# One dummy product per step on TensorE, from step 9 to step 54 of the attention of group 0

## The chip, the cores and the metric

The kernel runs on one NeuronCore of a Trainium2 chip. The metric is the device time of one execution in microseconds (us); lower is better. The kernel before takes 572.56 us, the median of three runs (572.24 to 572.80).

## The reference

Three blocks follow one another.

1. Causal attention over 2 batches, 12 heads, 448 positions and 64 values per head: `scores = q kT / 8`, the upper triangle masked, `exp(scores - max)` divided by its row sum, times `v`. The result becomes `x`, 896 tokens by 768.
2. `h = x @ w_in` (768 to 2048), `g = h * clip(h + 3, 0, 6) / 6`, `x = g @ w_out` (2048 to 768).
3. RMS norm of `x` with a gain vector, then `silu(xn @ w_gate) * (xn @ w_val)` (768 to 1536 twice) and `@ w_out` (1536 to 768).

The weights come as 64-bit floats; the products have to be as good as 32-bit ones.

## The kernel before, in words

The sequence is cut in two halves of 224 positions. Group 0 is the first half of all sequences, group 1 the second. Attention works in units of two heads of one batch: units 0 to 11 are group 0 (112 x 224 scores at most), units 12 to 23 are group 1 (112 x 448 at most). After attention a product is written as three: high half times high half, high times low, low times high (`mm3`, lines 209, 211 and 213), each 128 x 128 weights by 448 columns.

The order of all instructions is written out by hand in *steps*. In each step the loop at the end of the kernel first issues what has come due (`due`: masks, exponentials, evictions, each so many steps after what it needs), then the entries of `plan` for this step in order of their priority number, then some products of the dense layers. The products start at step 67 (`products_from`) and only then; so TensorE, which works in program order, comes to the first of them when everything of steps 0 to 66 is done. Engines do not stop between steps: a step is only a place in the order.

Unit `u` starts at step `5 u`. The stages of a unit of group 0, by line:

- **s** (line 319, TensorE): four score products, each in two passes, so eight matmul rows. Two heads use the upper and the lower 64 rows of the array. Entry `a_scores` at step 5u.
- mask and row minimum (329, VectorE), two steps later; **exp** and row sums (336, ScalarE), two steps after that; reciprocal of the sums (343, 344, VectorE); scaling (354, GpSimd).
- **t** (370, TensorE): three transposes of 112 x 112 for each of two heads, entry `a_transpose` at steps 5u + 15 and 5u + 16.
- **pt** (380, ScalarE): the copy of a transposed tile out of PSUM.
- **o** (396, TensorE): four products with `v` in eight passes, entry `a_values` at step 5u + 22; then the split of the result (406 ScalarE, 412 VectorE).

Units 8 to 11 have shorter distances (tables `SUMS`, `TRANSPOSES`, `VALUES`, `LAG`), so that the last value products of group 0 are at step 64. From step 23 on, five steps of group 0 hold on TensorE: t and s, then t, then o, then two steps with nothing. ScalarE also prepares the first weights in this time: `narrowed` (line 160) and `w_halves` (185) from steps 26, 38 and 50.

All results of TensorE go through one pool of eight PSUM banks (`psum`). One of its tiles is `warm`: `warm_up(n)` (line 933) issues n products of a 128 x 128 tile of ones by itself into it, and nothing reads it. Before, it is called six times over at the very start and once at each of steps 1, 3, 6 and 8. A bank goes back to the pool when the last instruction that uses its tile is issued in the written order.

Of the kernel before, what the change touches and what calls it, by code (L numbers as in the profile page):

```python
# [51 lines left out]
def fused_kernel(ctx: ExitStack, tc, qa, qb, ka, kb, v, w_in, w_out, w_gate, w_val, w_out2, rms_g, out):  # L52
# [13 lines left out]
    def psum(name):  # L66
        return pspool.tile([128, 512], F32, tag="ps", name=name)
# [27 lines left out]
    def begin_step():  # L95
        now = clock["now"]
        while due[now]:
            fn, args = due[now].pop(0)
            fn(*args)
        del due[now]  # L100

    def end_step():
        clock["now"] += 1
# [167 lines left out]
    NA = NU // 2  # L271
    ld, lv, sm, st, pt, xs = {}, {}, {}, {}, {}, {}

    def phase(u):
        return {NA - 1: 2, NU - 1: 2, NA - 2: 3, NA - 3: 4, NA - 4: 5}.get(u, units[u][0])
# [637 lines left out]
    def products():  # L913
        yield from ff1_in(0, 0)
        plan_preps(0, *PREPS[0])
        yield from ff1_in(1, NP1)
        yield from ff1_out(0, 2 * NP1)
        at(1, w_split)
        plan_preps(PREPS[0][2], *PREPS[1])
        pair_early(PLAIN)  # L920
        yield from ff1_out(1, 3 * NP1)
        yield from ff2_plain(IN2)
        yield from ff2_strassen()
        yield from strassen(OUT2)

    with tc.manual_schedule():
        nc.vector.memset(ones, 1.0)

        warm = psum("warm")

        def warm_up(n):
            for _ in range(n):
                nc.tensor.matmul(warm[:, :128], ones, ones, start=True, stop=True)

        warm_up(6)
        make_identity(nc, ident)
        nc.gpsimd.memset(mask, 0.0)
        nc.gpsimd.affine_select(
            out=mask[:, S - C:], in_=mask[:, S - C:], compare_op=ALU.is_ge, fill=MASK,
            base=0, pattern=[[-1, C]], channel_multiplier=1)  # L940
        nc.gpsimd.memset(half, 0.5)
        nc.gpsimd.memset(eps, 1e-6)


        plan = defaultdict(list)

        def start(u):
            return 5 * u

        for n in (1, 3, 6, 8):  # L950
            plan[n].append((4, warm_up, 1))
        for u in range(NU):
            s0 = start(u)
            ahead = max(0, NA + 4 - u) if u >= NA else 0
            plan[max(0, s0 - (24 if u < NA else 6 + 4 * ahead))].append((0, a_load, u))
            t0, o0 = s0 + TRANSPOSES[phase(u)], s0 + VALUES[phase(u)]
            plan[o0 - 12].append((0, a_load_v, u))
            plan[s0].append((3, a_scores, u))
            for j in range(2):
                plan[t0 + j].append((3, a_transpose, u, j))  # L960
            plan[o0].append((3, a_values, u))
        products_from = max(start(u) + VALUES[phase(u)] for u in range(NA)) + 3
        plan[0].append((1, lambda: nc.sync.dma_start(gvec, rms_g.rearrange("(k p) -> p k", p=128))))
        for n in range(3):
            plan[12 + 12 * n].append((1, w_load))
            plan[52 + 6 * n].append((1, w_load))
        for n in range(3):
            plan[26 + 12 * n].append((0, w_split))

        work = products()  # L970
        live = True
        attention_until = max(start(u) + VALUES[phase(u)] for u in range(NU)) + 3
        quota = 0.0
        while live or any(plan.values()) or any(due.values()):
            begin_step()
            now = clock["now"]
            for _, fn, *args in sorted(plan.pop(now, []), key=lambda e: e[0]):
                fn(*args)
            if now >= products_from and live:
                quota += BESIDE if now < attention_until else AFTER  # L980
                while quota >= 1 and live:
                    quota -= 1
                    if next(work, 0) == 0:
                        live = False
            end_step()
# [56 lines left out]
```

## Time and profile before

| | |
|---|---|
| median of three runs | 572.56 us |
| the profiled execution | 572.75 us |
| its span, first to last instruction | 571.0 us |
| mean granted TensorE clock | 0.996 of full |
| TensorE busy (matmul rows) | 562.2 us, 98% of the span |
| VectorE busy | 410.4 us, 72% |
| ScalarE busy | 390.6 us, 68% |
| GpSimd busy | 85.5 us, 15% |

All views come from one profiled execution. A timeline row gives the start and the length of a merged run of like instructions. Matmul rows overlap: the end of one is modelled and reaches past the start of the next, so what a group costs TensorE is best read from start to next start. PE is TensorE's matmul, PEld its weight load, DVE VectorE, ACT ScalarE, POOL GpSimd, SPq the DMA queue of SyncE. A clock of 1.00 is 2.4 GHz and 0.50 is 1.2 GHz. The share of busy time hides that the kernel has stages: up to about 47 us there is attention of group 0 alone, and afterwards dense products, with attention of group 1 in between.

### The profile page before, as it was taken

Reading aid. Unit: us, or ns where it says so; the run is one execution under the profiler, and the core shown is the slowest. Engines: PE = TensorE matmul, PEld = TensorE weight load, DVE = VectorE, ACT = ScalarE, POOL = GpSimd, SP = SyncE. Lnnn points to the kernel's source line nnn. Section 1 sums busy time; section 2 is a strip of 40 time slices with the busy share of each in tenths; the row PEclk is TensorE's granted clock in tenths of the full one; section 3 lists DMA queues with packets and bytes.
Section 4 is the critical chain, followed back from the end, with each engine's and each line's share of the span. In section 5 each row is a group of like instructions: output and inputs, shape, how many; then the busy total and the mean of one; then the engine's idle time right before and its main releaser. Section 6 shows DMA issues by size and latency. Waiting matters only on the chain.

```text
span 571.0 us, 9072 instructions
## 1 busy us (share of the span) xinstructions
PE 562.2 (98%) x3048; PEld 491.8 (86%) x3048; DVE 410.4 (72%) x796; ACT 390.6 (68%) x766; POOL 85.5 (15%) x130
## 2 busy tenths in 40 slices
PE   8899999999999999999999999999999999999997
PEld 6556777777899999999999999999999999999996
DVE  4676686867558857555589869969886876966861
ACT  6997878787667766877487767486667664754430
POOL 4665636362200000001001100000000000000000
PEclk9999999999999999999999999999999999999999
DMA  8958767664266997997789923037744607585841
GB/s 226 275 155 280 232 224 228 212 215 142 64 238 211 318 357 259 322 344 257 265 292 383 398 106 143 10 118 264 260 157 179 223 33 260 184 280 198 274 145 64
DMA packets 51231, 125.59 MB, mean 220 GB/s; under 512 B 6768, under 2 KB 30256, under 8 KB 51184
## 3 DMA queue, kind: packets, MB, share of 16 engines
q1 hardware_dynamic: 50752, 124.66, 63.6%
q8 instruction: 24, 0.39, 0.3%
q10 hardware_dynamic: 432, 0.34, 0.2%
q14 instruction: 23, 0.19, 0.1%
HBM read 93.36 MB, written 31.62 MB: 219 GB/s over the span
## 4 chain that ended last, share of the span: by engine, by line
PE 95%; ACT 3%; DMA 1%; SPq 0%; issue 0%; DVE 0%
PE y L209 8%; PE y L213 8%; PE y L211 8%; PE h L213 7%; PE h L209 7%; PE h L211 7%; PE f L209 5%; PE f L213 5%; PE f L211 5%; PE s L319 4%; PE o L396 4%; PE t L370 4%; PE fx L209 2%; PE fr L213 2%; PE fx L213 2%; PE fr L211 2%
## 5 line engine op out<-in xcount | busy, mean ns | idle before, releaser
L191 DVE TENSOR_TENSOR wlo<-c,whi 128x768 fp32r<-128x768 f32 x89 | 88.9, 1003 | 19.7 <-ACT whi L185 18.0
L185 ACT CAST whi<-c 128x768 fp32r<-128x768 f32 x89 | 74.0, 834 | 37.9 <-DVE c L169 18.0
L213 PE MATMUL h<-xh,wlo 128*128 128x448 f32 x192 | 72.0, 375 | 0.0
L211 PE MATMUL h<-xl,whi 128*128 128x448 f32 x192 | 70.9, 369 | 0.0
L209 PE MATMUL y<-ghi,whi 128*128 128x448 f32 x192 | 70.6, 367 | 0.0
L209 PE MATMUL h<-xh,whi 128*128 128x448 f32 x192 | 70.4, 367 | 0.0
L213 PE MATMUL y<-ghi,wlo 128*128 128x448 f32 x192 | 70.0, 365 | 0.0
L211 PE MATMUL y<-glo,whi 128*128 128x448 f32 x192 | 69.3, 361 | 0.0
L354 POOL TENSOR_SCALAR sm<-sm,st 112x112 f32<-112x112 f32 (+1 forms) x96 | 55.6, 598 | 69.3 <-ACT pt L380 28.3
L336 ACT ACTIVATE sm<-sm,st 112x112 f32<-112x112 f32 (+3 forms) x96 | 49.8, 530 | 4.3 <-DVE st L329 4.3
L169 DVE SCALAR_TENSOR_TENSOR c<-c,raw 128x768 uint32<-128x768 uint32 x36 | 36.5, 1015 | 17.4 <-ACT raw L164 10.7
L213 PEld LDWEIGHTS h<-xh,wlo 128*128 128x128 f32 x192 | 36.0, 188 | 9.3 <-issue 6.7
L329 DVE CUSTOM_DVE_ANT_0 sm<-s,mask 112x112 f32<-112x112 f32 (+3 forms) x96 | 37.3, 442 | 7.9 <-PE s L319 7.6
L433 DVE SCALAR_TENSOR_TENSOR t<-t,h 128x448 f32<-128x448 f32 x32 | 19.7, 616 | 27.1 <-ACT t L429 27.0
L213 PEld LDWEIGHTS y<-ghi,wlo 128*128 128x128 f32 x192 | 35.9, 187 | 3.6 <-issue 0.2
L211 PEld LDWEIGHTS h<-xl,whi 128*128 128x128 f32 x192 | 36.0, 188 | 2.8
L211 PEld LDWEIGHTS y<-glo,whi 128*128 128x128 f32 x192 | 36.0, 188 | 2.7
L209 PEld LDWEIGHTS h<-xh,whi 128*128 128x128 f32 x192 | 36.2, 188 | 2.5
L209 PEld LDWEIGHTS y<-ghi,whi 128*128 128x128 f32 x192 | 36.0, 188 | 2.5 <-issue 0.2
L429 ACT ACTIVATE t<-h,half 128x448 f32<-128x448 f32 x32 | 20.4, 636 | 25.3 <-PE h L213 25.3
L370 PE MATMUL t<-ident,sm 112*112 112x112 f32 x240 | 32.9, 268 | 2.7 <-POOL sm L354 2.3
L600 POOL TENSOR_TENSOR sq<-sq,sq 128x448 f32<-128x448 f32 x8 | 10.1, 1258 | 170.1 <-ACT sq L589 164.5
(174 smaller groups left out, 1351.9 us busy)
## 6 DMA issues: line engine op xcount, KB each, us to landing
raw<-in_w_in SPq DMA_DIRECT2D x16, 768.0 KB, 5.4
raw<-in_w_out SPq DMA_DIRECT2D x16, 768.0 KB, 6.3
braw<-in_w_out SPq DMA_DIRECT2D x12, 768.0 KB, 6.1
c<-kept SPq DMA_DIRECT2D x21, 384.0 KB, 3.1
a<-left SPq DMA_DIRECT2D x35, 224.0 KB, 3.9
praw<-in_w_gate SPq DMA_DIRECT2D x10, 768.0 KB, 4.5
praw<-in_w_val SPq DMA_DIRECT2D x10, 768.0 KB, 5.9
keptin<-c SPq DMA_DIRECT2D x16, 384.0 KB, 2.7
```

The source lines that it names most:

```text
L169: nc.vector.scalar_tensor_tensor(bits, bits, 3, z, ALU.logical_shift_left, ALU.bitwise_or)
L185: nc.scalar.copy(hi, c)
L191: nc.vector.tensor_sub(lo, c, f32(hi))
L209: nc.tensor.matmul(ps, whi, xhi, start=first, stop=False, skip_group_check=again)
L211: nc.tensor.matmul(ps, whi, xlo, start=False, stop=False, skip_group_check=again)
L213: nc.tensor.matmul(ps, wlo, xhi, start=False, stop=last, skip_group_check=again)
L319: nc.tensor.matmul(ps[:C, o:o + n], tq[64 * j:64 * j + 64, i * C:(i + 1) * C], tk[64 * j:64 * j + 64, 0:n], start=True, stop=True)
L329: nc.vector.tensor_tensor_reduce(dst, src, mask[:, S - n:], scale=-0.125, scalar=3e38, op0=ALU.add, op1=ALU.min, accum_out=st[u][:, 0, c:c ...
L336: nc.scalar.activation(dst, dst, AF.Exp, scale=-1.0, bias=st[u][:, 0, c:c + 1], accum_out=st[u][:, 1, c:c + 1])
L354: nc.gpsimd.tensor_scalar(t[:, o:o + n], t[:, o:o + n], c, 1.0, op0=ALU.mult, op1=ALU.mult)
L370: nc.tensor.transpose(banks[-1][:C, o:o + C], t[:, o0 + kc * C:o0 + (kc + 1) * C], ident[:C, :C])
L396: nc.tensor.matmul(ps[64 * j:64 * j + 64, HS - n:HS], tv[:, kc, 64 * j:64 * j + 64], t[:, o:o + n], start=kc == 0, stop=kc == nk - 1)
```

## The change

`warm_up(1)` is planned once more at each of steps 9 to 54 (`start(NA - 1)` is 55), 46 times in all, with priority 2: after the loads of its step and before its score, transpose and value products (priority 3).

```diff
         for n in (1, 3, 6, 8):
             plan[n].append((4, warm_up, 1))
+        for n in range(9, start(NA - 1)):
+            plan[n].append((2, warm_up, 1))
         for u in range(NU):
```

Nothing else is edited. The tile `warm` is now used until step 54 rather than step 8, and so is its PSUM bank.

## Rows read from the trace of the kernel before

**Rows 1.** Page: busy time by engine, and the chain of waits by engine.
```profile
PE 562.2 (98%) x3048; PEld 491.8 (86%) x3048; DVE 410.4 (72%) x796; ACT 390.6 (68%) x766; POOL 85.5 (15%) x130
PE 95%; ACT 3%; DMA 1%; SPq 0%; issue 0%; DVE 0%
```

**Rows 2.** Busy time by stage: engines (x instructions), clock, DMA share, GB/s.
```profile
8.18:34.14 25.96, 22.66 (x184) 14.14 (x183) 18.64 (x106) 25.92 (x101) 18.41 (x41) 0.93 0.81 241
34.14:47.05 12.91, 11.93 (x90) 7.22 (x90) 8.71 (x34) 11.27 (x41) 8.38 (x16) 1.00 0.79 238
47.05:571.00 523.95, 520.49 (x2744) 464.77 (x2742) 381.28 (x644) 350.10 (x617) 57.20 (x65) 1.00 0.63 219
27.66:31.07 3.41, 3.41 (x20) 2.00 (x19) 2.45 (x16) 3.41 (x15) 1.97 (x6) 0.50 0.76 220
```

**Rows 3.** Waits of TensorE, whole run: us in total, times, longest.
```profile
PE t L370 <- POOL sm L354: 2.3, 3, 1.4
PE o L396 <- DMA v<-in_v: 0.4, 1, 0.4
PE s L319 <- ACT pt L380: 0.2, 1, 0.2
```

**Rows 4.** Timeline of TensorE, group 0 at full clock: start, length, what.
```profile
11.93 0.83 PE L319 MATMUL s<-k,q 64*112 64x112 f32 x8
12.69 0.50 PE L370 MATMUL t<-ident,sm 112*112 112x112 f32 x3
13.12 0.79 PE L396 MATMUL o<-pt,v 112*64 112x224 f32 x8
13.85 0.50 PE L370 MATMUL t<-ident,sm 112*112 112x112 f32 x3
14.28 0.83 PE L319 MATMUL s<-k,q 64*112 64x112 f32 x8
```

**Rows 5.** The tile of the dummy products, whole run: ns min/median/max.
```profile
L933 PEld LDWEIGHTS warm<-ones x20: 186/333/334, 1.0 to 7.9; 128*128 128x128 f32 x20
L933 PE MATMUL warm<-ones x20: 275/421/582, 1.0 to 8.0; 128*128 128x128 f32 x20
```

**Rows 6.** Timeline of weight loads: two dummy products, then scores, full clock.
```profile
7.54 0.52 PEld L933 LDWEIGHTS warm<-ones 128*128 128x128 f32 x4 [0.29 <-issue]
...
8.18 0.37 PEld L319 LDWEIGHTS s<-k,q 64*112 64x112 f32 x6
```

**Rows 7.** Timeline of weight loads: last transpose of seven, then dense products.
```profile
48.45 0.14 PEld L370 LDWEIGHTS t<-ident,sm 112*112 112x112 f32 x1
48.55 0.19 PEld L211 LDWEIGHTS h<-xl,whi 128*128 128x128 f32 x1
48.66 0.19 PEld L213 LDWEIGHTS h<-xh,wlo 128*128 128x128 f32 x1
```

**Rows 8.** Timeline of TensorE around the dense products' start.
```profile
47.76 0.37 PE L209 MATMUL h<-xh,whi 128*128 128x448 f32 x1
47.97 0.84 PE L370 MATMUL t<-ident,sm 112*112 112x112 f32 x7
```

**Rows 9.** Timeline of TensorE, units 10 to 13: scores, the first dense product.
```profile
31.50 0.83 PE L319 MATMUL s<-k,q 64*112 64x112 f32 x8
...
34.14 0.83 PE L319 MATMUL s<-k,q 64*112 64x112 f32 x8
...
44.92 1.57 PE L319 MATMUL s<-k,q 64*112 64x336 f32 x8
46.42 0.88 PE L370 MATMUL t<-ident,sm 112*112 112x112 f32 x7
47.07 0.45 PE L209 MATMUL h<-xh,whi 128*128 128x448 f32 x1
```

**Rows 10.** Timeline of ScalarE: exponentials of unit 10, and of unit 12.
```profile
33.55 0.42 ACT L336 ACTIVATE sm<-sm,st 112x112 f32<-112x112 f32 x1
...
35.15 0.22 ACT L336 ACTIVATION_READ_ACCUMULATOR sm<-sm,st 112x1 f32 x1
35.24 0.45 ACT L380 COPY pt<-t 112x336 f32<-112x336 f32 x1
...
40.66 0.64 ACT L336 ACTIVATE sm<-sm,st 112x336 f32<-112x336 f32 x1
```

**Rows 11.** Timeline of TensorE through the stretch at half clock.
```profile
22.85 0.45 PE L319 MATMUL s<-k,q 64*112 64x112 f32 x2
23.49 0.83 PE L319 MATMUL s<-k,q 64*112 64x112 f32 x6 [0.20 <-ACT pt L380]
...
26.87 0.83 PE L370 MATMUL t<-ident,sm 112*112 112x112 f32 x3 [1.40 <-POOL sm L354]
27.62 1.46 PE L319 MATMUL s<-k,q 64*112 64x112 f32 x8
29.02 0.81 PE L370 MATMUL t<-ident,sm 112*112 112x112 f32 x3
29.76 1.39 PE L396 MATMUL o<-pt,v 112*64 112x224 f32 x8
31.08 0.50 PE L370 MATMUL t<-ident,sm 112*112 112x112 f32 x3
```

## The prediction, made before the result was known

> **What bounds the kernel now.** I read the page's engine shares and its chain of waits first: TensorE is busy 98% and carries 95% of the chain [rows 1]. That is an average over two stages, so I cut the span where the dense products begin. From 47.05 us to the end TensorE is busy 520.49 of 523.95 us at full clock [rows 2]; nothing of the change is in there, and the written order fixes it, so that part moves as a block: whatever delays the first dense product at 47.07 us [rows 9] delays the end by as much, one to one. The question is only when TensorE gets there.
>
> The steps that receive dummies run, on TensorE, from the scores of unit 2 (the step 10 scores, 8.18 us [rows 6]) to the scores of unit 11 (step 55, 34.14 us [rows 9]): 25.96 us. In that stretch ScalarE is busy 25.92 us, without a gap [rows 2]; it is the bound. TensorE's busy 22.66 us there is not work at its pace, as matmul rows overlap. Read from start to next start, at full clock, scores of one unit cost 0.76 us (11.93 to 12.69), three transposes 0.43 us, a value group 0.73 us [rows 4]. Steps 9 to 54 hold nine score groups (units 2 to 10), eighteen transpose groups (units 0 to 8, two each) and seven value groups (units 0 to 6): 9 x 0.76 + 18 x 0.43 + 7 x 0.73 = 19.7 us. So TensorE has 25.96 - 19.7 = 6.3 us to spare, part of it as plain waits, mostly for the scaled rows from GpSimd [rows 3], part as a stretch at half clock [rows 11].
>
> **The change part by part.** It removes nothing. It adds 46 dummy products.
>
> *Price of one.* The ten dummies of before show as twenty loads and twenty matmuls, so each is two passes [rows 5]. At full clock two dummies run from 7.54 us to the next group's first load at 8.18 us: 0.64 us for four passes [rows 6]. The four loads are done in 0.52 us with the last one 0.19 us long [rows 5, 6], so a pass follows the last after (0.52 - 0.19) / 3 = 0.11 us; four take 0.43 us, and 0.21 us are left for the change to the scores. One dummy is thus 0.215 us of pace, and the question is whether each *run* of dummies (those with nothing between them) also pays 0.21 us. Runs: six up to step 22 (steps 9-10, 11-15, 16, 17-20, 21, 22), three in each of the six units of steps 23 to 52 (three dummies, one, one), and one each at 53 and 54; that is 26 runs and 14 + 30 + 2 = 46 dummies.
>
> - Lower end: 46 x 0.215 = 9.9 us.
> - Upper end: 9.9 + 26 x 0.21 = 15.4 us.
>
> The pause of 0.21 us lies at a change between the full array and the scores' two half-arrays. At a change between transposes and other full-array work there is none: the load after the last transpose starts 0.10 us after it, the same spacing as between loads around it [rows 7], and a transpose follows a dense product after 0.21 us, which is that product's own length [rows 8]. A run of dummies always stands next to transposes or between groups that change the array's layout anyway (scores to transposes, value products to transposes), so it adds hardly a pause of its own. I take 0.02 us a run: 9.9 + 0.5 = 10.4 us, near the lower end.
>
> The Trainium skill ("TensorE: Matmul & The Clock Gate", Single matmul latency) says that a lone matmul cannot hide its drain and costs (398 + N) / 2.4 ns when warm, 219 ns for these 128 columns, where a stream pays only its columns. An estimate from that page, if it held for all 92 passes, is 20.2 us, and the sum would end at 585.3 us; if only each run's last pass drained in the open, it comes to about the upper end, which is rival 1. The trace sides with the stream within a run (0.11 us a pass) [rows 6] and leaves the run's end open.
>
> *What it does in the stretch.* TensorE's own work becomes 19.7 + 10.4 = 30.1 us, against 25.96 us taken now. ScalarE no longer sets the pace: TensorE does, 4.1 us later at step 55. ScalarE then has 4.1 us of slack over the stretch, but its load is uneven (about 0.9 us of weight preparation now and then), so a little waiting stays: between nothing and the 2.9 us of waits of now [rows 3]; I take 0.3 us, near nothing, since transposes come five steps or more after their scaling is issued and a step is now about 0.65 us.
>
> *The clock.* TensorE falls to 1.2 GHz from 27.66 to 31.07 us [rows 2], after it had sat 1.40 us waiting for GpSimd [rows 11]. In it scores took 1.40 us for 0.76, transposes 0.74 for 0.43, value products 1.32 for 0.73: some 1.5 us. ScalarE was busy 3.41 of those 3.41 us [rows 2], so the half clock costs the kernel nothing now. My sum already takes full clock throughout; if the fall stayed, 1.5 us would come on top. I expect it to go, as no such wait is left.
>
> *What is given back behind step 55.* From 34.14 to 47.07 us no dummies run: 12.93 us. Now ScalarE comes into this part late: unit 10's exponentials end at 35.24 us, 3.74 us after its scores and 1.10 us *after* unit 11's scores start [rows 9, 10]. With the dummies, unit 11's scores come 2.64 + 4 x 0.235 = 3.6 us after unit 10's, and ScalarE, no longer behind, ends those exponentials by about then. ScalarE works without a pause from there to unit 12's exponentials at 40.66 us [rows 10] and these lead to the last value products, so its lead carries over: 1.2 us given back. Bounds: nothing, and 2.3 us, at which TensorE's own work in this part (scores of units 11, 12 and 13 at 0.76, 1.50 and 1.50 us, six transpose groups at 0.43 and one at 0.65, five value groups at 0.73 [rows 4, 9]: 10.6 us) would bind.
>
> *Banks.* `warm` holds a PSUM bank up to step 54, leaving seven. Each unit takes five. TensorE has waited for a bank 0.20 us in this stretch with eight [rows 11]; as it is now the late one, I put this at nothing. Loads, DMA queues and other engines gain no instruction; they are paced by TensorE and shift with it.
>
> *Sum.* 4.1 + 0.3 - 1.2 = +3.2 us. The profiled execution takes 572.75 us (1.75 us around its span of 571.0), 0.19 us above the median of the runs; on the median, 572.56 + 3.2 = **575.8 us**. Own range of this case: 573.9 (lower price, no waits, 2.3 us given back: +1.3) to 577.5 (waits of 2 us).
>
> **Rivals.**
>
> 1. *Every run pays its change of layout.* 19.7 + 15.4 = 35.1 us, +9.1 in the stretch, less 1.2: 580.5 us. For it: the 0.21 us stands in the only place where dummies were timed. Against it: transposes next to dense products show no pause [rows 7, 8].
> 2. *Seven banks.* Scores wait for a copy out of PSUM in each unit. One such copy on ScalarE is 0.45 us [rows 10]; nine units at 0.4 us are 3.6 us on top of the forecast: 579.4 us. For it: the one wait of that kind [rows 11]. Against it: TensorE will be behind the copies, not ahead of them.
> 3. *Not slower: the dummies fall into the pauses.* If a dummy between scores and transposes fills the pause of about 0.2 us that is there anyway, 26 runs save up to 5 us, the dummies cost 9.9 - 5.2 = 4.7 us, and TensorE's 24.4 us stay under the 25.96 of ScalarE: 572.6 us, at best some tenths less. It decides at a price of 6.3 / 46 = 0.136 us a dummy for no delay at step 55, or, with the 1.2 us given back, 0.163 us. For it: 6.3 us to spare is much. Against it: even in a stream a dummy takes 0.215 us [rows 6], and dummies between two transposes find no pause.
> 4. *It does not do what it says.* Dummies could be dropped as dead. All ten of before are in the trace [rows 5]; so hardly.
>
> **How the numbers follow.** Forecast 0.60, rival 1 0.13, rival 2 0.11, rival 3 0.13, rival 4 and the rest 0.03. The predicted time is the forecast's. The range has to reach into rivals 1 and 2 above and to the edge of rival 3 below: 573.2 to 580.5 us. A measurement of this kernel can tell about 0.2% (1.1 us) from no change, so "same" is 571.4 to 573.7 us. Rivals 3 and 4 fall in it, with 0.04 of chance just below it; a sliver of the forecast's low end does too. Faster 0.04, same 0.13, slower 0.83.
>
> **What would show it.** In the changed profile: 112 matmul rows of the dummies (20 + 92); pairs 0.21 to 0.24 us apart from neighbours; unit 11's scores at about 38.5 us and the first dense product at about 50.3 us; ScalarE with some 4 us of gaps before step 55 and TensorE without waits there; no half clock; the block after it as long as before, 524 us. Wrong would be: dummies that cost 0.4 us when alone (rival 1), scores that wait for PSUM copies (rival 2), or ScalarE still full and unit 11's scores near 34 us (rival 3).

## The result and the profile after

The changed kernel takes 575.79 us (median of four runs, 575.05 to 576.49) against 572.40 us for the kernel before (median of four, with one run more than the 572.56 us that the forecast started from): a ratio of 1.0059, 95% interval 1.0041 to 1.0076. It is 3.4 us slower; 3.2 us slower, 575.8 us, was forecast. Its profiled execution took 575.05 us, span 573.3 us.

Busy time by stage of the changed kernel, columns as in [rows 2]: from unit 2's scores to unit 11's, from there to the first dense product, and the rest.

```profile
7.32:37.51 30.19, 30.19 (x272) 23.74 (x271) 18.84 (x105) 28.28 (x109) 19.74 (x42) 1.00 0.71 214
37.51:49.33 11.82, 10.82 (x90) 6.81 (x90) 8.02 (x34) 9.55 (x33) 7.18 (x15) 1.00 0.79 247
49.33:573.30 523.97, 520.49 (x2744) 464.74 (x2742) 381.48 (x644) 350.78 (x617) 57.19 (x65) 1.00 0.63 219
```

Read it against [rows 2]. The stretch with dummies grew from 25.96 to 30.19 us. In it TensorE is now busy all the time, and ScalarE, which was busy 25.92 of 25.96, has 1.9 us free (28.28 of 30.19). The part behind it shrank from 12.91 to 11.82 us. The dense block is as long as before, 523.97 against 523.95. The waits of TensorE over the whole run, columns as in [rows 3], say the same: none is left in the stretch. The two that remain lie at the very start (up to 1.05 us) and behind the stretch (before the value products at 46.13 us); the kernel before has both as well, 1.0 us each, beside the three of [rows 3].

```profile
PE warm L933 <- DVE ones L927: 1.1, 1, 1.1
PE o L396 <- ACT pt L380: 1.0, 1, 1.0
```

The timeline of TensorE for one unit of the changed kernel, to be read from start to next start beside [rows 4]:

```profile
14.78 0.94 PE L933 MATMUL warm<-ones 128*128 128x128 f32 x6
15.55 0.45 PE L370 MATMUL t<-ident,sm 112*112 112x112 f32 x3
15.94 0.83 PE L319 MATMUL s<-k,q 64*112 64x112 f32 x8
16.70 0.49 PE L933 MATMUL warm<-ones 128*128 128x128 f32 x2
17.02 0.45 PE L370 MATMUL t<-ident,sm 112*112 112x112 f32 x3
17.31 0.40 PE L933 MATMUL warm<-ones 128*128 128x128 f32 x2
17.64 0.79 PE L396 MATMUL o<-pt,v 112*64 112x224 f32 x8
18.36 0.38 PE L933 MATMUL warm<-ones 128*128 128x128 f32 x1
```

Three dummies take 0.77 us, a single one 0.32 or 0.33 us. But the transposes between two dummies now take 0.29 us where they took 0.43 next to scores and value products [rows 4]: the pause at a change of array layout, between products on the full array and those on half-arrays, moved; it was not paid twice. The unit lasts 3.58 us (14.78 to 18.36); without dummies its groups come to 2 x 0.43 + 0.76 + 0.73 = 2.35 us. That leaves 1.23 us for five dummies, 0.25 us each. All 112 matmul rows of the dummies (20 and 92) are in the trace, which leaves nothing of rival 4.

At the start the two profiled executions differ by something else. First the kernel before, then the changed one, TensorE up to unit 2's scores:

```profile
5.30 1.22 PE L933 MATMUL warm<-ones 128*128 128x128 f32 x4
6.46 1.16 PE L319 MATMUL s<-k,q 64*112 64x112 f32 x8
7.54 0.71 PE L933 MATMUL warm<-ones 128*128 128x128 f32 x4
8.19 0.83 PE L319 MATMUL s<-k,q 64*112 64x112 f32 x8
```

```profile
4.83 0.71 PE L933 MATMUL warm<-ones 128*128 128x128 f32 x4
5.47 0.83 PE L319 MATMUL s<-k,q 64*112 64x112 f32 x8
6.23 1.16 PE L933 MATMUL warm<-ones 128*128 128x128 f32 x8
7.32 0.83 PE L319 MATMUL s<-k,q 64*112 64x112 f32 x8
```

The same four passes of dummies start 0.47 us earlier in the second and take 0.64 us to the next start, against 1.16 us in the first. The clock column of the profile reads 1.00 here in both; from the pace, the second is at 2.4 GHz by then and the first still at 1.2 GHz. So unit 2's scores start 0.87 us earlier in the changed kernel, although two dummies more (steps 9 and 10) stand before them: 1.09 us from the dummies to the scores instead of 0.65. The profiled pair therefore shows +4.23 - 1.09 - 0.87 + 0.02 = +2.3 us of span. An estimate for a pair in which the clock rises at the same moment: the two dummies show as +0.44 (1.09 - 0.65), and 4.23 + 0.44 - 1.09 = +3.6 us, beside +3.4 us of the medians.

### The profile page after: what moved, and what is told of

Same layout as the page of the kernel before. It is cut to its first block, busy times and chain, and to the rows that moved or that the text cites. A ratio compares the mean times of both kernels' runs of the same rounds, so it can differ in the third digit from the quotient of the medians.

```text
span 573.3 us, 9257 instructions
## 1 busy us (share of the span) xinstructions
PE 567.8 (99%) x3140; PEld 500.5 (87%) x3140; DVE 410.6 (72%) x796; ACT 391.8 (68%) x766; POOL 85.6 (15%) x130
## 4 chain that ended last, share of the span: by engine, by line
PE 98%; ACT 1%; issue 0%; DVE 0%; ACTq 0%
PE y L209 8%; PE y L213 8%; PE y L211 8%; PE h L213 7%; PE h L209 7%; PE h L211 7%; PE f L209 5%; PE f L213 5%; PE f L211 5%; PE s L319 5%; PE o L396 4%; PE t L370 4%; PE warm L933 3%; PE fr L213 2%; PE fx L209 2%; PE fx L213 2%
## 5 line engine op out<-in xcount | busy, mean ns | idle before, releaser
L160 ACT ACTIVATE c<-raw 128x768 f32<-128x768 f32 x36 | 32.9, 915 | 2.1 <-DMA raw<-in_w_gate 1.5
```

The source lines that it names most:

```text
L160: nc.scalar.activation(c, f32(high), AF.Prelu, scale=2.0 ** -112, alpha=2.0 ** 32)
```

## The experiments

Each kernel was timed in rounds together with the kernel before, whose median in those rounds was 572.3 to 572.6 us. "The stretch" is from unit 2's scores to unit 11's. A run of dummies is, as in the prediction, dummies with nothing between them. Edits are against the kernel before where nothing else is said.

**The bank alone.**

```diff
+        plan[54].append((2, warm_up, 1))
```

> One dummy, at step 54 alone, so that the dummies' PSUM bank is held as long as in the changed kernel but TensorE has 0.2 us more to do. Theory (TensorE's added work): 572.4 us, within 0.4 of the kernel before, the stretch from unit 2's to unit 11's scores stays near 26.0 us. Rival (seven banks instead of eight): scores wait for copies out of PSUM, up to 3.4 us slower, 574 to 576 us.

572.06 us, ratio 0.9996 (0.9987 to 1.0005). Holding the PSUM bank up to step 54 costs nothing here. In this kernel ScalarE is still the late one and could hide a wait of TensorE for a bank (its longest for a copy, before scores, is 0.56 us); but in the changed kernel TensorE waits for no copy in the stretch either, as shown above. Rival 2 is out. The stretch, columns as in [rows 2]:

```profile
7.13:33.28 26.15, 21.79 (x185) 13.80 (x184) 18.53 (x106) 26.11 (x103) 18.91 (x41) 1.00 0.84 249
```

**Half of the dummies.**

```diff
+        for n in range(10, start(NA - 1), 2):
+            plan[n].append((2, warm_up, 1))
```

> 23 dummies, at the even steps 10 to 54. Theory (TensorE's sum against ScalarE's): TensorE's work in the stretch is 19.7 + 23 x 0.23 = 25.0 us, still under ScalarE's 25.9, so the time stays within 0.8 us of before: 572.4 to 573.2. Rival (each dummy costs its share wherever it stands): half of 3.4 us, 574.1.

572.38 us, ratio 0.9998 (0.9989 to 1.0007). The 23 dummies, 22 of them in the stretch, are free within some 0.6 us, so the cost is not a share per dummy. The stretch is at the edge: TensorE 25.66 and ScalarE 25.58 of 25.86 us.

```profile
7.98:33.84 25.86, 25.66 (x227) 18.68 (x226) 18.05 (x106) 25.58 (x100) 18.86 (x41) 1.00 0.83 246
```

**The same 46 in 10 runs instead of 26.**

```diff
+        for n in range(13, start(NA - 1), 5):
+            plan[n].append((2, warm_up, 5))
+        plan[54].append((2, warm_up, 1))
```

> 46 dummies as in the changed kernel, but five at a time at steps 13, 18, ..., 53 and one at 54: 10 runs instead of 26. Theory (a price per dummy, 0.215 us, hardly any per run): 575.4, within 0.6 of the changed kernel. Rival (a price per run, 0.21 us each): 16 runs fewer, 3.4 us less, 572.4.

575.36 us, ratio 1.0048 (1.0035 to 1.0060). The stretch takes 30.11 us, nearly as in the changed kernel, although all 46 dummies lie in it instead of 44. With a dummy at 0.223 us (next run), the 15 runs fewer in it save 0.5 us, 0.035 us each and not 0.21. What is paid is the dummy, hardly the run; rival 1 is out.

```profile
6.97:37.08 30.11, 30.11 (x276) 23.46 (x275) 19.60 (x108) 29.16 (x111) 20.00 (x42) 1.00 0.79 223
```

**Twice the dummies** (edit against the changed kernel).

```diff
         for n in range(9, start(NA - 1)):
-            plan[n].append((2, warm_up, 1))
+            plan[n].append((2, warm_up, 2))
```

> 92 dummies, two at each of steps 9 to 54, in the same 26 runs. Theory: beyond the point where TensorE binds each further dummy costs its whole 0.215 us: 46 x 0.215 = 9.9 us over the changed kernel, 585.7 (584.7 to 586.0, as ScalarE's lead may give back a little more behind step 55). Rival (runs are what is paid): 576 to 577. Rival (part of the price is made up by the clock, already full): no difference from the theory.

586.06 us, ratio 1.0237 (1.0223 to 1.0251): 10.3 us over the changed kernel for 46 more, 0.22 us each. The stretch takes 40.01 us.

```profile
8.60:48.61 40.01, 40.01 (x359) 33.58 (x358) 19.10 (x103) 28.50 (x105) 21.66 (x46) 1.00 0.53 156
```

Forty-four of the 46 dummies of the changed kernel lie in the stretch, and 88 of the 92 here: (40.01 - 30.19) / 44 = 0.223 us a dummy. What is left of the changed kernel's stretch over TensorE's 19.7 us, 10.5 - 44 x 0.223 = 0.7 us, makes 0.03 us for each of 25 runs.

**The clock alone.**

```diff
+        for n in range(39, 51):
+            plan[n].append((2, warm_up, 1))
```

> 12 dummies, one at each of steps 39 to 50, around the place where TensorE waited 1.40 us and its clock then fell to half for 3.4 us. TensorE has room for them (19.7 + 2.7 = 22.4 us against 25.9 of ScalarE). Theory (ScalarE binds there, the half clock cost nothing): no half clock if the wait is filled, and still 572.4, within 0.4. Rival (the half clock cost its 1.5 us): 570.9.

572.30 us, ratio 0.9992 (0.9979 to 1.0006). In its profiled execution the granted clock was 1.00 throughout the stretch, and nothing was gained; the 1.5 us of the rival lie outside the interval.

```profile
7.52:33.33 25.81, 23.48 (x208) 16.18 (x207) 18.72 (x106) 25.77 (x101) 18.76 (x41) 1.00 0.86 250
```

The kernel with the bank alone says more: in its profiled execution the clock stayed full too, with the wait still there.

```profile
26.14 0.83 PE L370 MATMUL t<-ident,sm 112*112 112x112 f32 x3 [1.31 <-POOL sm L354]
26.91 0.83 PE L319 MATMUL s<-k,q 64*112 64x112 f32 x8
```

The stretch is as long with the half clock (25.96 us) as without it (25.81 and 26.15). The half clock of the kernel before, under which ScalarE was busy all the time [rows 2], cost nothing that shows.

The whole executions differ more. Of 75 runs of the kernel before, timed beside the experiments, the 24 with a mean granted clock of 1.00 and the 12 with 0.997 have a median of 572.0 us, the 38 with 0.993 to 0.996 one of 572.6 (one more, at 0.985, took 577.2). In the profiles the difference lies at the start: unit 2's scores come at 8.19 us in the kernel before (mean clock 0.996) and at 7.13 with the bank alone (1.00), and the first dense product at 47.07 and 46.35. That this holds for all 38 is not shown.

**Copies of head 0 on VectorE, without and with dummies.**

```diff
-            nc.scalar.copy(t, bank[:C, :w])
+            if units[u][0] == 0 and j == 0:
+                nc.vector.tensor_copy(t, bank[:C, :w])
+            else:
+                nc.scalar.copy(t, bank[:C, :w])
```

> The kernel before, with the copies of head 0's transposes out of PSUM (group 0 only) on VectorE instead of ScalarE: 12 copies, of which 9 in the stretch, at 0.33 us from start to start. Theory (ScalarE binds the stretch before the change): 1.5 to 3.5 us faster, 569 to 571 us. Rival (the stretch was bound by TensorE or by the chain of one unit through the engines): 572.4.

571.74 us, ratio 0.9990 (0.9971 to 1.0009): not told apart from before, and less than was expected. The stretch shows why: ScalarE fell to 23.80 us of work, but the stretch only to 25.56.

```profile
8.21:33.77 25.56, 22.09 (x184) 13.68 (x183) 21.82 (x114) 23.80 (x95) 18.39 (x41) 0.93 0.83 244
```

The likely reason is that VectorE now has the copies in its order and makes the reciprocals later: the waits of GpSimd's scaling for them total 16.2 us from 8 to 46 us, where they were 10.0 (first the kernel before, then this one). No run tests this by itself. The half clock of this stretch (27.5 to 31.0 us) is not the reason: ScalarE is busy all through it, 3.50 of 3.50 us.

```profile
POOL sm L354 <- DVE st L344: 10.0, 5, 7.1
POOL sm L354 <- DVE st L344: 16.2, 9, 7.1
```

> The changed kernel with the same copies on VectorE. Theory (with the dummies TensorE binds the stretch, not ScalarE): no gain in the stretch, at most 0.7 us behind it: 575.1 to 575.8. Rival (ScalarE still binds, slowed by its waits for TensorE): as much faster as without dummies, 572.5 to 574.

575.15 us, ratio 1.0044 (1.0028 to 1.0060). The edit is the same, in the changed kernel. The stretch is 30.19 us, to the hundredth that of the changed kernel, with 3 us less on ScalarE.

```profile
8.18:38.37 30.19, 30.19 (x272) 23.74 (x271) 21.64 (x113) 25.36 (x98) 19.37 (x42) 1.00 0.69 208
```

**No row sums on ScalarE, without and with dummies.** This takes work from ScalarE and gives none to another engine; the row sums of group 0 are left out.

```diff
-                accum_out=st[u][:, 1, c:c + 1])
+                **({} if units[u][0] == 0 else {"accum_out": st[u][:, 1, c:c + 1]}))
...
-        nc.vector.tensor_scalar_add(t[:, 2], t[:, 1], 1e-9)
+        nc.vector.tensor_scalar_add(t[:, 2], t[:, units[u][0]], 1e-9)
```

> The kernel before without the row sums of group 0's exponentials (their place in the scaling is taken by the row minimum): ScalarE loses one short read of 0.09 us per exponential, 37 in the stretch, 3.4 us, and no other engine gains work. Leaves out the sums of group 0. Theory (ScalarE binds the stretch): 2 to 4 us faster, 568.4 to 570.4. Rival (the chain of one unit through VectorE and GpSimd binds as closely as ScalarE, as moving the copies to VectorE suggests with 0.4 us gained for 3.0 moved): 571.5 to 572.2.

570.11 us, ratio 0.9964 (0.9951 to 0.9978). ScalarE did bind the stretch: it falls to 24.78 us. But of 3.4 us taken away only 1.2 us came out of it against the kernel before (25.96), 1.4 against the bank alone (26.15), and ScalarE waits now (23.62 busy of 24.78). Its waits are 0.6 us for TensorE's transposes, 0.3 for VectorE's masks and 0.2 for a weight load. The half clock is in this profiled execution too, from 25.1 to 28.5 us, but ScalarE is busy all through it, 3.41 of 3.41 us.

```profile
7.08:31.86 24.78, 21.68 (x184) 13.78 (x183) 18.45 (x106) 23.62 (x67) 18.28 (x41) 0.93 0.91 265
```

> The changed kernel, likewise without the row sums of group 0. Theory (with the dummies TensorE alone binds the stretch): the stretch keeps its 30.2 us; only behind it up to 0.7 us can go: 575.0 to 575.8. Rival (ScalarE still has a share in the 30.2 us): 572 to 574.

575.36 us, ratio 1.0056 (1.0043 to 1.0068). The stretch is again 30.19 us. What gains 2.2 us without the dummies gains some 0.4 with them, and nothing of it in the stretch.

```profile
7.38:37.57 30.19, 30.19 (x272) 23.74 (x271) 18.86 (x105) 24.82 (x68) 19.69 (x42) 1.00 0.73 215
```

**Dummies of 64 columns** (edit against the changed kernel).

```diff
-        def warm_up(n):
+        def warm_up(n, w=128):
...
-                nc.tensor.matmul(warm[:, :128], ones, ones, start=True, stop=True)
+                nc.tensor.matmul(warm[:, :w], ones, ones[:, :w], start=True, stop=True)
...
-            plan[n].append((2, warm_up, 1))
+            plan[n].append((2, warm_up, 1, 64))
```

> The changed kernel with dummies of 64 columns instead of 128 at steps 9 to 54, their weights 128 x 128 as before. If the load of the weights sets the pace of a dummy (0.107 us a pass), nothing changes: 575.4 to 576.0. If the columns set it, a dummy costs 0.107 us, all 46 some 5 us; TensorE's sum is then 25.1 us, under ScalarE's 25.9, and the time is that of before, 572.3 to 573. The prediction's sum needs only the price, so it says nothing on which; the kink does: a halved price must bring the whole 3.4 us back.

574.00 us, ratio 1.0030 (1.0019 to 1.0042): neither of the two. The stretch is 28.86 us, 1.33 us shorter, which is 0.053 us for each of 25 runs and not 0.107 for each dummy.

```profile
7.66:36.52 28.86, 28.86 (x271) 22.79 (x270) 18.57 (x105) 27.70 (x107) 19.32 (x42) 1.00 0.75 222
```

A run of three takes 0.71 us (14.86 to 15.57) instead of 0.77, a single dummy 0.27 (10.74 to 11.01) instead of 0.32: the saving is the same for both.

```profile
10.74 0.43 PE L933 MATMUL warm<-ones 128*128 128x64 f32 x2
11.01 0.45 PE L370 MATMUL t<-ident,sm 112*112 112x112 f32 x3
...
14.86 0.88 PE L933 MATMUL warm<-ones 128*128 128x64 f32 x6
15.57 0.45 PE L370 MATMUL t<-ident,sm 112*112 112x112 f32 x3
```

Inside a run the pace is that of the weight loads, 0.11 us a pass, whatever the columns (the six loads of a run of three take 0.74 us in both kernels); the columns count only in its last pass. The Trainium skill ("TensorE: Matmul & The Clock Gate", LDWEIGHTS (loading the stationary operand)) gives a load as its columns divided by 1.2, in ns, 107 ns for 128; the 0.11 us a pass here agree.

**A version that beats both.** GpSimd has some 7 us to spare in the stretch of the kernel before [rows 2], and VectorE's order seems the sore point. So the high halves of the first three weight tiles went to GpSimd.

```diff
-        nc.scalar.copy(hi, c)
+        if n < 3:
+            nc.gpsimd.tensor_copy(hi, c)
+        else:
+            nc.scalar.copy(hi, c)
```

> The kernel before, with the high halves of the first three weight tiles (three copies of 128 x 768, 0.83 us each on ScalarE, two of them in the stretch) made on GpSimd, which is idle for 7 of the 26 us. Theory (ScalarE binds the stretch, the chain through the other engines follows 1.3 us behind): 0.5 to 1.8 us faster, 570.6 to 572.0, unless the copy on GpSimd takes over 1.5 us and holds up the scaling. Rival (GpSimd's scaling is as late as ScalarE): 572.3 or slower, up to 573.5.

570.86 us, ratio 0.9982 (0.9973 to 0.9991) to the kernel before: 1.5 us faster than it and 4.9 us faster than the changed kernel. A copy takes 0.82 us on GpSimd, as much as on ScalarE, and the stretch falls to 25.07 us. The time goes with the clock here: the six runs at a mean granted clock of 0.999 took 570.4 to 570.9 us, the three at 0.993 or 0.994 took 572.0 to 572.5. With less on ScalarE a half clock may cost something; no run separates that from a later rise at the start.

```profile
L186 POOL CAST whi<-c x3: 817/817/824, 19.5 to 36.5; 128x768 fp32r<-128x768 f32 x3
```

```profile
6.96:32.03 25.07, 21.48 (x183) 13.43 (x183) 18.79 (x106) 24.79 (x101) 19.48 (x42) 1.00 0.92 264
```

## Why the prediction was right

- *The dense block moves as a block.* Right: 523.97 us against 523.95.
- *The price of a dummy.* 0.215 us and 0.02 us a run were taken; the doubled kernel gives 0.223 and 0.03. The reading that a run next to transposes pays hardly a pause of its own held: 10 runs or 26 take the same 30.1 to 30.2 us. The lone-matmul latency of the Trainium skill ("TensorE: Matmul & The Clock Gate", Single matmul latency), weighed there and given by the page for bf16, did not apply: at 219 ns a pass a dummy would be 0.44 us. Its weaker form does not come to the upper end either: 219 instead of 108 ns for the last pass of 26 runs adds 2.9 us to 9.9, which is 12.8 and not 15.4.
- *TensorE's sum against ScalarE's.* 30.1 us and 0.3 us of waits were taken for the stretch; it was 30.19 us with no wait. That is a little flattering: the two dummies of steps 9 and 10 lie before unit 2's scores and were counted in the stretch, so that the dummies in all cost 30.19 + 0.44 - 25.96 = 4.7 us, not 4.4. The kink is shown by the runs: 23 dummies cost nothing, 46 cost 3.4 us, each of the next 46 costs its full price, and relief for ScalarE, which gains 2.2 us without the dummies, changes the stretch with them by nothing. Where the kink lies is an estimate: drawn back from 46 at 0.223 us a dummy, the 3.4 us are used up at some 31 dummies.
- *ScalarE as the bound before.* Right, but by less than "without a gap" suggested: with 3.4 us less to do it yields some 1.3 us in the stretch, and then it waits 1.1 us for others, TensorE's transposes first; that the order of VectorE and GpSimd is behind this is likely and not shown. The prediction did not need this margin; a forecast of an edit that relieves ScalarE would have.
- *Given back behind step 55.* 1.2 us taken, 1.09 measured. The mechanism is in ScalarE's timeline of the changed kernel, beside [rows 10]: unit 10's exponentials end by 36.88 us, before unit 11's scores at 37.51 rather than 1.1 us after; ScalarE even waits for unit 11's mask; and unit 12's exponentials start 5.45 us after unit 11's scores instead of 6.52.

```profile
35.09 0.39 ACT L336 ACTIVATE sm<-sm,st 112x112 f32<-112x112 f32 x1
...
36.69 0.19 ACT L336 ACTIVATION_READ_ACCUMULATOR sm<-sm,st 112x1 f32 x1
...
38.75 0.39 ACT L336 ACTIVATE sm<-sm,st 112x112 f32<-112x112 f32 x1 [0.64 <-DVE st L329]
...
42.96 0.61 ACT L336 ACTIVATE sm<-sm,st 112x336 f32<-112x336 f32 x1
```

- *The clock.* The half clock went, as expected, and was worth nothing that shows, as expected. That it goes *because* no wait is left was argued and is not shown: the execution with the bank alone had the wait and no half clock.
- *Where the profile disagreed.* The first dense product was forecast at about 50.3 us and came at 49.35, with unit 11's scores at 37.51 rather than 38.5. The lengths were right; the starting point moved, as the clock rose earlier in this execution. ScalarE was to have some 4 us of gaps in the stretch and has 1.9: as it is no longer behind, 2.4 us of its work that lay behind step 55 now lie before it (28.28 us busy, 25.92 before). That is the same lead that is given back, seen from its other side, and the prediction did not carry it over to this sign. A dummy alone stands 0.32 us from the group behind it, not 0.21 to 0.24, as the pause before that group now lies there.
- *The number.* The mechanism was right; that 575.8 meets 575.79 is luck. The changed kernel's own runs spread over 1.4 us. Against the medians +3.2 is short by 0.2 us, which the lower median of the kernel before (572.40 for 572.56) makes up. Among the terms, the dummies cost some 0.5 us more in all than was taken and 0.1 us less was given back, while 0.3 us of waits were not there.

## What to carry to other kernels

Filling an engine's idle time is free only up to the point where its own work reaches the time that another engine sets; add up both over the stretch first, from start to next start, and the answer is a kink, not a rate. Here TensorE's spare time of 6.3 us had room for some 25 dummies in the stretch, some 30 with what is given back behind it, and got 46. A low clock on an engine is no loss to be bought back as long as another engine is busy all the time under it, as ScalarE was here. Work that has to go is better moved to an engine with time to spare, and a run has to show that nobody waits for its order: three copies on GpSimd gained 1.5 us, twelve on VectorE nothing that shows.

## What the runs showed of the hardware

- TensorE's clock rises at different moments of the same instructions: after the same twelve passes of dummies and eight of scores, the next four passes of dummies took 1.16 us to the next start in the kernel before and 0.64 with the bank alone (1.2 and 2.4 GHz by the pace). In kernels that are alike up to there, unit 2's scores started between 6.96 us (high halves on GpSimd) and 8.19 (before). So single profiles should be compared by the lengths of stretches, not by positions.
- The fall to 1.2 GHz in the middle came in the kernel before after a wait of 1.40 us and did not come, in the kernel with the bank alone, after a wait of 1.31 us at the same place.
- Halving the columns of a dummy saved 0.053 us a run and nothing within a run, where the loads of its weights followed each other after 0.11 us with 64 columns as with 128.
